# Band attention, SiLU feed-forward and a top-1 mixture of experts in one kernel: the first slots, chunk zero, unit one's transposes and the first expert loads are put in another order

## The chip, the cores and the metric

The kernel runs on one core of a Trainium2 chip. The metric is the device time of one execution in microseconds (us). The kernel before was timed three times: 567.33, 568.43 and 568.99 us, median 568.43 us.

## The reference, cut to what matters

Three stages follow each other on B = 2 sequences of S = 768 tokens, 8 heads of 64 (1536 tokens of 512 values).

```python
# 1 attention: 8 global keys, a local band of 96, a slope per head
scores = q @ k.T / 8 + (-slope[h] * dist)
scores = where(is_global | is_local, scores, -1e9)
a = exp(scores - max); a /= a.sum() + 1e-9
x = (a @ v)                       # 1536 x 512
# 2 feed-forward, 512 -> 2048 -> 512
h = x @ w_in
x = (h * sigmoid(h)) @ w_out
# 3 top-1 mixture of 8 experts, 512 -> 1024 -> 512
e_idx = argmax(x @ w_gate)
y = relu(x[mask] @ w1[e]) @ w2[e]
out[mask] = softmax_weight * sigmoid(x @ w_output_gate)[e] * y
```

## The kernel before

The 1536 tokens are 12 tiles of 128 (n = 0 to 11) and six units of two tiles. Attention is cut into **slots**: slot s = 4n + hp does the two heads 2hp and 2hp+1 of tile n. Slots 0 to 23 (`slot_b`) run ahead of the feed-forward, with fp32 matrix products: the scores (`emit_qk`, L173), scores plus the bias table with their maximum on VectorE (`emit_tb`, L183), the exponential on ScalarE (`emit_exp`, L194), three slots later the transposes (`emit_tr`, L213) and their copies out of PSUM (`emit_cp`, L219 on VectorE, L220 on ScalarE), and one slot after that the product with the values (`emit_px`, L230). At a tile's end the row sums are inverted (`emit_rs`), spread over 512 columns by GpSimd (L1014, `rx`), transposed (`emit_rb`, L237), copied by ScalarE (L239, `xn`) and multiplied into the result (`emit_xx`); GpSimd writes the feed-forward's input from it (`put_xt`, L277 and L279). Slots 24 to 47 (`slot`) run inside the feed-forward, with fp16 pairs (`emit_h` L198, `emit_l` L201 and L204, a DMA transpose on SyncE's queue, `emit_pv` L254, `emit_fin` L264, `emit_xt` L271, then L278 and L279).

The bias tables are built at the very start. `params` asks for the two band sizes, `spread` converts them (L89) and copies them to all partitions with a small matmul (`pfb`, L91) and L92; `table_floats` converts index grids (L116 on VectorE, L117 on ScalarE); `table` makes three VectorE steps (L123 to L125), once for the 128-wide slice of a sequence's first tile and once for the other three slices (384 wide); `tab_heads` scales a table for a head, even heads on ScalarE (L129) and odd ones on VectorE (L128). TensorE is kept at work meanwhile by `warm` (L83), matmuls of a matrix of ones whose result nothing reads.

The feed-forward runs in five chunks of 16 steps: chunk 0 has units 0 and 1, chunks 1 to 4 one unit each. Step g does the first product (`s1_mm`, L355, 12 matmuls a unit), tanh and product (L359, L360), the split into two parts (`s1_sp`, L363 on ScalarE, L364 on VectorE), and two steps later the second product (`s2_mm`, L375 to L377, with `wolr` tiles that `load_wol`, L344, fetches). Everything else is put between these by the step loop (L1093 to L1145), an order written out by hand: slots put their parts in a list that `run_ev` empties, gating functions sit in a list that `run_gates` empties one a step. `slot_b` of drain slots 24 to 27 (the last slots' tails) falls in the first steps of chunk 0; `gate_consts` (L387 to L405, constants on GpSimd and the load of `wgs`) stands ahead of chunk 0. A unit of chunks 1 to 3 is turned for gating by `turn`, which sets two DMA transposes (L439, L440) on SyncE's queue per tile; `gate3` ranks tokens by small matmuls (L477 to L479) and `gate4` scatters rows into expert order (L500).

In chunk 4 `moe2_pre` asks step by step for the first 16 tiles of expert weights (`load_u`, L563, 256 KB each) and splits them (`split_u`: L568 on ScalarE, L569 on VectorE); `early_load` (L577, L579) fetches the first expert's rows after the scatter. All these loads and the `wolr` ones are issued by SyncE, in order. Then `moe2` runs the experts.

Of the kernel before, what the change touches and what calls it, by code (L numbers as in the profile page):

```python
# [17 lines left out]
ALU = mybir.AluOpType  # L18
# [5 lines left out]
def kernel(ctx, tc, qk, v, n_global, n_local, w_in, w_out, wg, w1, w2, out):  # L24
# [33 lines left out]
    tabs=attn.tile([P,4,H,P],BF16,name="tabs")  # L58
# [54 lines left out]
    def table_floats(k,e):  # L113
        w,ii,jj=tabm['w']
        for o,i in ((w[:,0,k],ii[:,k]),(w[:,1,k],jj[:,k])):
            if e is V: V.tensor_copy(o,i)  # L116
            else: A.activation(out=o,in_=i,func=AF.Copy)  # L117
    def table(k):

        w=tabm['w'][0]  # L120
        rel,col,loc,a=(w[:,i,k] for i in range(4))
        ng=pf[:,0:1]; nl=pf[:,2:3]
        V.tensor_scalar(out=loc,in0=rel,scalar1=nl,scalar2=BIG,op0=ALU.is_ge,op1=ALU.mult)  # L123
        V.scalar_tensor_tensor(out=loc,in0=col,scalar=ng,in1=loc,op0=ALU.is_ge,op1=ALU.mult)
        V.scalar_tensor_tensor(out=a,in0=rel,scalar=nl,in1=loc,op0=ALU.min,op1=ALU.add)  # L125
    def tab_heads(dst,src,hs):
        for h in hs:
            if h%2 if dst.start<3 else h<2: V.tensor_scalar(out=tabs[:,dst,h,:],in0=tabm['w'][0][:,3,src],scalar1=-8.0*2.0**-(h+1),scalar2=None,op0=ALU.mult)  # L128
            else: A.activation(out=tabs[:,dst,h,:],in_=tabm['w'][0][:,3,src],func=AF.Copy,scale=-8.0*2.0**-(h+1))  # L129

    atags=[['a','s20','s21','s22','s23']]; acnt=[0]; ded=[False]
# [4 lines left out]
    raw={}; vraw={}; kb={}; qs={}; vp={}; tt={}; hl={}; pT={}; pvt={}; mx={}; ss={}; xT={}  # L136
    def load(s):
        n,hp=divmod(s,4); b,i=divmod(n,NT); r=ring[hp//2]; z=ksl(n)
        if n==0: A.dma_start(r[:,hp%2,z],qk[b,i,hp//2,:,hp%2])
        elif hp%2==0: S.dma_start(r[:,:,z],qk[b,i,hp//2])  # L140
    def load_v(n):
            b,i=divmod(n,NT)
# [73 lines left out]
    def emit_cp(y,m,e):  # L216
        for r in range(2):
            o=y[:,:,:,r*D:(r+1)*D]
            if e is V: V.tensor_copy(o,m[r])  # L219
            else: A.activation(out=o,in_=m[r],func=AF.Copy)  # L220
# [535 lines left out]
    def moe2_pre(k):  # L756

        q=[(q,i) for q in (0,2,1,3) for i in range(KC)]
        w=(0,0,2,2,2,3,3,1,1,2)
        if 6<=k<16:  # L760
            for _ in range(w[k-6]): split_u(*q[nq[1]],pool=False); nq[1]+=1
            while nq[0]<min(16,nq[1]+4*(k-5),nq[1]+NQR): load_u(*q[nq[0]]); nq[0]+=1
        if k==6: early_iota()
        if k==7: early_load()
        if k==8: early_rows()
        if k==13: early_prep()
# [216 lines left out]
    def own(n): return 4*(n+2)>=SB  # L983
    def slot_b(s):
# [19 lines left out]
        def a2():  # L1004
            if cur: emit_tb(n,hp,1)
            if o3: emit_cp(*cp[0],A if DQ<=s<23 else V)
            if o3 and h3==3 and own(n3): emit_rb(n3)
            if o4: emit_px(n4,h4)
            if o4 and h4==3 and not own(n4): emit_rb(n4)
            if o5 and h5==3 and not own(n5): emit_xx(n5)  # L1010
            if o2 and h2==3:
                for k in range(2): emit_rs(n2,k)
                r=attn.tile([P,512],F32,tag="t",name="rx",bufs=3)
                G.tensor_copy(r.rearrange("p (h d) -> p h d",h=H),rs[n2].to_broadcast([P,H,D])); rs[n2]=r  # L1014
        ev.append(a2)
        def b_():
            if cur: glob_k(n,hp)
            if h4==3 and o4 and own(n4): emit_xx(n4)
            if s==0: table(slice(0,3))
            for d,h in TB.get(s,()): tab_heads(slice(0,2) if d==0 else slice(2,3),slice(0,2) if d==0 else slice(2,3),(h,))  # L1020
            if hp==3 and 4*(n+1)<SB and cur: load_v(n+1)
        ev.append(b_)
# [43 lines left out]
    with tc.manual_schedule():  # L1066
        params()
        want(7); load_v(0)
        table_ints()
        warm(6)  # L1070
        spread()
        warm(2)
        table_floats(slice(3,4),V)
        table(slice(3,4))
        table_floats(slice(0,3),A)
        tab_heads(slice(3,4),slice(3,4),range(H))
        rows_init()
        s=0
        while s<SB:
# [4 lines left out]
            s+=1  # L1084
            for x in WP.get(s,()): w_to(*x)
        atags[0]=['s20','s21','s22','s23']
        gate_consts()

        steps=[(c,f) for c in range(len(CH)) for f in range(FB)]
        pend=[]  # L1090
        gq=[]
# [4 lines left out]
        for g in range(len(steps)+LAG):  # L1096
            live=g<len(steps)
            if live:
# [4 lines left out]
                for u in CH[c]: s1_mm(u,f)  # L1103
                for u in CH[c]: s1_ev(u,f)
                if c==0:
                    for _ in range(2):
                        if s<SB+4: pend+=slot_b(s); s+=1
                    if g==3: atags[0]=['a']
                    if f==FB-1: s=SB
                elif c<4 and s<NS+4 and (f>1 and f!=8 if c==1 else f%2==0):  # L1110
                    pend+=slot(s); s+=1
                run_ev(2 if c<2 else 1)
                for u in CH[c]: s1_sp(u,f)
# [6 lines left out]
            if g>=LAG:  # L1120
# [3 lines left out]
                if f2==FB-1:  # L1124
# [3 lines left out]
                    at=len(gq)  # L1128
                    for u in CH[c2]:
                        seq=[lambda n=n,fn=turn if u in PU else gate1: fn(n) for n in (2*u,2*u+1)]  # L1130
                        if u==1: seq=[lambda n=n,h=h: turn(n,(h,)) for n in (2,3) for h in (0,1)]
                        if u in PU: seq=[lambda u=u,fn=fn: fn(u) for fn in (piece1,piece2,piece3,piece4)]+seq+[lambda: None]*2
                        seq+=[lambda u=u,fn=fn: fn(u) for fn in (gate2,gate3,lambda u: gate4(u,1))]
                        for i,fn in enumerate(seq):
                            if at+i<len(gq): gq[at+i]=lambda fs=(gq[at+i],fn): [f() for f in fs]
                            else: gq.append(fn)
                        at=len(gq)-(4 if u in PU else 0)
# [76 lines left out]
```

## Time and profile before

| what | value |
|---|---|
| median of three runs | 568.43 us |
| the profiled execution | 571.45 us, span of its instructions 569.7 us |
| TensorE matmul busy (PE) | 552.6 us, 97% of the span |
| weight load (PEld) | 469.5 us |
| VectorE (DVE) | 391.0 us |
| ScalarE (ACT) | 302.7 us |
| GpSimd (POOL) | 142.2 us |
| attention ahead of the feed-forward | 0 to about 43 us |
| chunk 0, chunks 1 to 3, chunk 4 | to about 136, 313, 366 us |
| experts | from there to the end |

An engine's busy time is the sum of its instructions' durations. In a row of a timeline the first number is the start, the second the time taken by the group, and the bracket tells how long the engine stood idle before it and what released it. PEld is TensorE's weight load, which runs beside its matmuls. SPq, ACTq and POOLq are the sequencers that issue DMAs.

### The profile page before, as it was taken

The page shows a single profiled execution, that of the slowest core. Times are in us where ns is not written, and L with a number is a line of the kernel's source. Part 1 is how long each engine was busy: PE and PEld are TensorE (multiplying, and loading weights), DVE is VectorE, ACT ScalarE, POOL GpSimd, SP SyncE. Part 2 cuts the span into 40 slices and gives each one's busy share as a digit, 9 for nine tenths or more (in the row PEclk, how much of TensorE's full clock was granted, in tenths as well). Part 3 has the DMA queues.
Part 4 walks back from the last instruction along what each step waited for, and adds up shares of the span by engine and source line. Part 5 has one row for each costly group of instructions (what it writes and reads, how often), then busy time and mean ns, then how long its engine had stood idle before and what let it go on. Part 6 is the DMA issues. An engine that isn't in the chain of part 4 may idle for free.

```text
span 569.7 us, 12001 instructions
## 1 busy us (share of the span) xinstructions
PE 552.6 (97%) x4027; PEld 469.5 (82%) x4027; DVE 391.0 (69%) x1143; ACT 302.7 (53%) x819; POOL 142.2 (25%) x193
## 2 busy tenths in 40 slices
PE   9999999999999999999999999999999999999992
PEld 4667998888888888888998988788887888888871
DVE  6995899996478757574735256647674966977940
ACT  6994444443545454434522325727655776877740
POOL 2686434444133313123201010210011010010011
PEclk9999999999999999999999999999999999999997
DMA  6776477796657986664394349319674867867500
GB/s 221 263 238 198 168 216 231 232 310 217 196 154 172 185 206 154 170 160 146 102 184 129 79 144 337 111 56 339 223 216 143 275 199 238 262 221 260 156 20 23
DMA packets 90731, 107.55 MB, mean 189 GB/s; under 512 B 39180, under 2 KB 53516, under 8 KB 90660
## 3 DMA queue, kind: packets, MB, share of 16 engines
q1 hardware_dynamic: 87892, 99.77, 59.4%
q0 software_dynamic: 2192, 6.39, 3.0%
q8 instruction: 34, 0.56, 0.4%
q10 hardware_dynamic: 576, 0.52, 0.3%
q14 instruction: 37, 0.30, 0.2%
HBM read 87.14 MB, written 17.66 MB: 184 GB/s over the span
## 4 chain that ended last, share of the span: by engine, by line
PE 79%; DMA 5%; DVE 5%; issue 4%; ACT 4%; POOL 1%; SPq 1%; POOLq 0%; DVEq 0%; ACTq 0%
PE s L355 21%; PE s L375 7%; PE s L376 7%; PE s L377 7%; PE h L698 5%; PE xy L173 4%; PE y L731 3%; PE y L732 3%; PE y L733 3%; PE h L699 3%; PE pv L254 2%; PE h L704 2%; PE px L230 1%; PE xy L213 1%; DMA out_dram<-y,ixt 1%
## 5 line engine op out<-in xcount | busy, mean ns | idle before, releaser
L355 PEld LDWEIGHTS s<-xT,wi 128*128 128x128 f32 x1152 | 146.7, 190 | 8.4 <-DVE g L364 3.8
L355 PE MATMUL s<-xT,wi 128*128 128x256 f32 x1152 | 152.9, 284 | 0.5 <-DVE g L364 0.5
L359 ACT ACTIVATE u<-s 128x256 f32<-128x256 f32 x96 | 35.4, 381 | 98.7 <-PE s L355 98.5
L360 DVE SCALAR_TENSOR_TENSOR s<-u,s 128x256 f32<-128x256 f32 x96 | 39.7, 426 | 66.3 <-ACT u L359 66.0
L375 PE MATMUL s<-woh,g 128*128 128x512 f32 x192 | 78.4, 408 | 0.4 <-ACT g L363 0.4
L569 DVE TENSOR_TENSOR uq<-qr,uq 128x512 fp32r<-128x512 f32 x112 | 74.4, 689 | 4.8 <-ACT uq L568 2.8
L376 PE MATMUL s<-woh,g 128*128 128x512 f32 x192 | 75.8, 395 | 0.0
L568 ACT ACTIVATE uq<-qr 128x512 fp32r<-128x512 f32 x112 | 66.6, 625 | 2.7 <-DMA qr<-in_w_dram 2.7
L655 POOL DMA_INDIRECT out_dram<-y,ixt x17 | 18.9, 1114 | 156.8 <-ACT y L744 117.2
L364 DVE TENSOR_TENSOR g<-s,g 128x256 fp32r<-128x256 f32 x96 | 39.1, 421 | 22.0 <-ACT g L363 17.9
L363 ACT ACTIVATE g<-s 128x256 fp32r<-128x256 f32 x96 | 35.6, 381 | 30.2 <-DVE s L360 30.2
L194 ACT ACTIVATE t<-t,mx 128x256 f32<-128x256 f32 (+1 forms) x96 | 46.1, 487 | 0.6 <-DVE mx L183 0.5
L375 PEld LDWEIGHTS s<-woh,g 128*128 128x128 f32 x192 | 36.3, 189 | 7.4 <-issue 1.7
L376 PEld LDWEIGHTS s<-woh,g 128*128 128x128 f32 x192 | 36.3, 189 | 5.5 <-DVE g L364 0.5
L377 PE MATMUL s<-wolr,g 128*128 128x512 f32 x128 | 39.8, 392 | 0.2 <-DMA wolr<-wlo_d 0.2
L711 DVE TENSOR_TENSOR h<-h,hs 128x192 f32<-128x192 f32 (+5 forms) x56 | 20.8, 372 | 25.3 <-ACT hs L710 25.2
L731 PE MATMUL y<-uq,hh 128*128 128x512 f32 (+1 forms) x88 | 36.7, 417 | 0.0
L732 PE MATMUL y<-uq,hh 128*128 128x512 f32 (+1 forms) x88 | 34.6, 393 | 0.0
L733 PE MATMUL y<-uq,hh 128*128 128x512 f32 (+1 forms) x88 | 34.6, 393 | 0.0
L713 ACT ACTIVATE hh<-h 128x192 fp32r<-128x192 f32 (+5 forms) x56 | 19.8, 353 | 26.5 <-DVE h L711 15.9
L698 PE MATMUL h<-xwT,uq 128*128 128x448 f32 (+5 forms) x144 | 32.5, 347 | 0.0
L716 DVE SCALAR_TENSOR_TENSOR hh<-h,hh 128x128 fp32r<-128x128 f32 (+4 forms) x88 | 23.2, 293 | 13.2 <-ACT hh L713 13.2
(271 smaller groups left out, 1041.1 us busy)
## 6 DMA issues: line engine op xcount, KB each, us to landing
qr<-in_w_dram SPq DMA_DIRECT2D x128, 256.0 KB, 4.1
wolr<-wlo_d SPq DMA_DIRECT2D x64, 256.0 KB, 3.3
wiraw<-in_w_in_dram SPq DMA_DIRECT2D x16, 512.0 KB, 5.0
wraw<-in_w_out_dram SPq DMA_DIRECT2D x13, 512.0 KB, 4.0
ring<-in_qk_dram SPq DMA_DIRECT2D x22, 256.0 KB, 3.9
xe<-xe SPq DMA_DIRECT2D x7, 792.0 KB, 6.2
wlo_d<-wol SPq DMA_DIRECT2D x16, 256.0 KB, 2.7
xw<-xe SPq DMA_DIRECT2D x15, 264.0 KB, 4.7
```

Of the source, the lines that this page charges most:

```text
L194: A.activation(out=t[:,j,:ce],in_=t[:,j,:ce],func=AF.Exp,scale=-1.0 if 4*n<SB else 0.125,bias=mx[n][:,h:h+1],accum_out=ss[n][:,h,0:1])
L355: T.matmul(t,w[:,ww,kc,:],x[:,xx,kc,:],start=(k==0),stop=(k==11)); k+=1
L360: V.scalar_tensor_tensor(out=t,in0=u,scalar=1.0,in1=t,op0=ALU.add,op1=ALU.mult)
L375: T.matmul(o,g[u][:,0,sl],wh,start=(f==0),stop=False)
L376: T.matmul(o,g[u][:,1,sl],wh,start=False,stop=False)
L377: else: T.matmul(o,g[u][:,0,sl],wl,start=False,stop=(f==FB-1))
L568: A.activation(out=t[:,0],in_=r,func=AF.Copy)
L569: (G if (i%2 if pool is None else pool) else V).tensor_tensor(out=t[:,1],in0=r,in1=t[:,0],op=ALU.subtract)
L698: for kc in range(KC): T.matmul(t[:,:2*W],uq[4*p+2*(f//4),kc][:,0,s],xwT[p,kc][:,:,:W],start=(kc==0),stop=False)
L731: T.matmul(o,hi,w[:,0],start=(f==0),stop=False)
L732: T.matmul(o,g[:,z:z+n],w[:,0],start=False,stop=False)
L733: T.matmul(o,hi,w[:,1],start=False,stop=(f==7))
```

## The change

The edits fall in five places.

1. **Start.** Four warm matmuls instead of six stand ahead of `spread` and four instead of two behind it; VectorE's conversions L116 go ahead of `spread`. The three steps of the 384-wide table, which stood together in slot 0, go one ahead of slot 0, one into slot 0, one into slot 1. The eight odd-head scalings of these slices move from VectorE to GpSimd. Two of the four first loads of `ring` move from ScalarE's queue to SyncE's.
2. **Slots.** For tiles 4 and 5 `emit_px` is issued ahead of `emit_rb`.
3. **Chunk 0.** The four drain slots come one, two and one to a step instead of two and two, and `gate_consts` is called in step 3.
4. **Chunk 1.** Steps 12 and 15 take no slot (before, step 8), so from there on every slot comes one place later; unit 1's four transposes are issued two at step 12 and two at step 15, instead of one at each of four steps.
5. **Chunk 4.** The limit on the expert tiles asked for is 2(k-4) at step k, where it was 4(k-5) more than the number split.

```diff
-    def table(k):
+    def table(k,steps=(0,1,2)):
...
-        V.tensor_scalar(out=loc,in0=rel,scalar1=nl,scalar2=BIG,op0=ALU.is_ge,op1=ALU.mult)
-        V.scalar_tensor_tensor(out=loc,in0=col,scalar=ng,in1=loc,op0=ALU.is_ge,op1=ALU.mult)
-        V.scalar_tensor_tensor(out=a,in0=rel,scalar=nl,in1=loc,op0=ALU.min,op1=ALU.add)
+        if 0 in steps: V.tensor_scalar(out=loc,in0=rel,scalar1=nl,scalar2=BIG,op0=ALU.is_ge,op1=ALU.mult)
+        if 1 in steps: V.scalar_tensor_tensor(out=loc,in0=col,scalar=ng,in1=loc,op0=ALU.is_ge,op1=ALU.mult)
+        if 2 in steps: V.scalar_tensor_tensor(out=a,in0=rel,scalar=nl,in1=loc,op0=ALU.min,op1=ALU.add)
...
-            if h%2 if dst.start<3 else h<2: V.tensor_scalar(out=tabs[:,dst,h,:],in0=tabm['w'][0][:,3,src],scalar1=-8.0*2.0**-(h+1),scalar2=None,op0=ALU.mult)
+            if h%2 if dst.start<3 else h<2: (G if dst.start<3 else V).tensor_scalar(out=tabs[:,dst,h,:],in0=tabm['w'][0][:,3,src],scalar1=-8.0*2.0**-(h+1),scalar2=None,op0=ALU.mult)
...
-        if n==0: A.dma_start(r[:,hp%2,z],qk[b,i,hp//2,:,hp%2])
+        if n==0: (A if hp<2 else S).dma_start(r[:,hp%2,z],qk[b,i,hp//2,:,hp%2])
...
-            while nq[0]<min(16,nq[1]+4*(k-5),nq[1]+NQR): load_u(*q[nq[0]]); nq[0]+=1
+            while nq[0]<min(16,2*(k-4),nq[1]+NQR): load_u(*q[nq[0]]); nq[0]+=1
...
+            if o4: emit_px(n4,h4)
             if o3 and h3==3 and own(n3): emit_rb(n3)
-            if o4: emit_px(n4,h4)
...
-            if s==0: table(slice(0,3))
+            if s==0: table(slice(0,3),(1,))
+            if s==1: table(slice(0,3),(2,))
...
-        warm(6)
+        warm(4)
+        table_floats(slice(3,4),V)
         spread()
-        warm(2)
-        table_floats(slice(3,4),V)
+        warm(4)
         table(slice(3,4))
         table_floats(slice(0,3),A)
         tab_heads(slice(3,4),slice(3,4),range(H))
+        table(slice(0,3),(0,))
...
-        gate_consts()
-
...
-                    for _ in range(2):
+                    for _ in range(2 if g==1 else 1):
                         if s<SB+4: pend+=slot_b(s); s+=1
-                    if g==3: atags[0]=['a']
+                    if g==3: atags[0]=['a']; gate_consts()
...
-                elif c<4 and s<NS+4 and (f>1 and f!=8 if c==1 else f%2==0):
+                elif c<4 and s<NS+4 and (f>1 and f not in (12,15) if c==1 else f%2==0):
...
-                        if u==1: seq=[lambda n=n,h=h: turn(n,(h,)) for n in (2,3) for h in (0,1)]
-                        if u in PU: seq=[lambda u=u,fn=fn: fn(u) for fn in (piece1,piece2,piece3,piece4)]+seq+[lambda: None]*2
+                        if u==1: seq=[lambda: None,seq[0],lambda: None,lambda: None,seq[1]]
+                        if u in PU: seq=[lambda u=u,fn=fn: fn(u) for fn in (piece1,piece2,piece3,piece4)]+seq+[lambda: None]*(1 if u==1 else 2)
```

On TensorE, at the start, where `pfb` is the matmul that spreads the band sizes, `wm` the warm ones and `xy` the first scores, the order before was:

```order
8 L83 MATMUL wm<-ones 128x512
9 L83 LDWEIGHTS ones
10 L83 MATMUL wm<-ones 128x512
11 L83 LDWEIGHTS ones
12 L83 MATMUL wm<-ones 128x512
13 L91 MATMUL pfb<-pf_136,onef 128x4
14 L83 LDWEIGHTS ones
15 L83 MATMUL wm<-ones 128x512
16 L83 LDWEIGHTS ones
17 L83 MATMUL wm<-ones 128x512
18 L173 MATMUL xy<-ring_76 128x128 x4
```

and with the change it is:

```order
8 L83 MATMUL wm<-ones 128x512
9 L91 MATMUL pfb<-pf_136,onef 128x4
10 L83 LDWEIGHTS ones
11 L83 MATMUL wm<-ones 128x512
12 L83 LDWEIGHTS ones
13 L83 MATMUL wm<-ones 128x512
14 L83 LDWEIGHTS ones
15 L83 MATMUL wm<-ones 128x512
16 L83 LDWEIGHTS ones
17 L83 MATMUL wm<-ones 128x512
18 L173 MATMUL xy<-ring_76 128x128 x4
```

Eight warm matmuls stand ahead of the first scores in both; `pfb` has moved up past two of them.

On TensorE, around the first steps of chunk 0 (`px` is the product with the values, `rb` the transposed row sums, L355 the feed-forward's first product, two rows a step), the order before was:

```order
95 L237 MATMUL rb<-ident,rx 128x128 x4
96 L230 MATMUL px<-pT_796,vpr 64x128 x4
97 L213 MATMUL xy<-ident,t 128x64 x8
98 L230 MATMUL px<-pT_831,vpr 64x128 x4
99 L355 MATMUL s_914<-xT,wi 128x256 x12
100 L355 MATMUL s_927<-xT,wi 128x256 x12
101 L213 MATMUL xy<-ident,t 128x64 x8
102 L230 MATMUL px<-pT_864,vpr 64x128 x4
103 L213 MATMUL xy<-ident,t 128x64 x8
104 L230 MATMUL px<-pT_956,vpr 64x128 x4
105 L355 MATMUL s_994<-xT,wi 128x256 x12
106 L355 MATMUL s_1007<-xT,wi 128x256 x12
```

and with the change:

```order
95 L230 MATMUL px<-pT_796,vpr 64x128 x4
96 L237 MATMUL rb<-ident,rx 128x128 x4
97 L213 MATMUL xy<-ident,t 128x64 x8
98 L230 MATMUL px<-pT_831,vpr 64x128 x4
99 L355 MATMUL s_883<-xT,wi 128x256 x12
100 L355 MATMUL s_896<-xT,wi 128x256 x12
101 L213 MATMUL xy<-ident,t 128x64 x8
102 L230 MATMUL px<-pT_864,vpr 64x128 x4
103 L355 MATMUL s_941<-xT,wi 128x256 x12
104 L355 MATMUL s_954<-xT,wi 128x256 x12
105 L213 MATMUL xy<-ident,t 128x64 x8
106 L230 MATMUL px<-pT_925,vpr 64x128 x4
```

`px` has moved ahead of `rb`, and one pair of transposes and product has moved from ahead of step 1's L355 rows to behind them.

On SyncE's queue in chunk 4 (`qr` is a tile of expert weights, `ex` and `exg` the scattered rows, an ISA row the register work ahead of an address), the order before was:

```order
173 L563 ISA
174 L563 DMA qr<-in_w_dram 128x512
175 L563 ISA
176 L563 DMA qr<-in_w_dram 128x512
177 L577 ISA
178 L577 DMA ex<-xe 128x528
179 L579 ISA
180 L579 DMA exg<-xe 128x2x528
181 L344 DMA wolr<-wlo_d 128x512
182 L563 ISA
183 L563 DMA qr<-in_w_dram 128x512
```

and with the change, where the rows shown begin at the earlier `wolr`:

```order
172 L344 DMA wolr<-wlo_d 128x512
173 L563 ISA
174 L563 DMA qr<-in_w_dram 128x512
175 L563 ISA
176 L563 DMA qr<-in_w_dram 128x512
177 L577 ISA
178 L577 DMA ex<-xe 128x528
179 L579 ISA
180 L579 DMA exg<-xe 128x2x528
181 L344 DMA wolr<-wlo_d 128x512
182 L563 ISA
183 L563 DMA qr<-in_w_dram 128x512
```

Ahead of `ex` there were eight `qr` requests and there are now six; the seventh and eighth have moved behind `exg` and a `wolr`.

## Rows read from the trace of the kernel before

**Rows 1.** The page, part 1: busy time, share of the span, instructions.
```profile
PE 552.6 (97%) x4027; PEld 469.5 (82%) x4027; DVE 391.0 (69%) x1143; ACT 302.7 (53%) x819; POOL 142.2 (25%) x193
```

**Rows 2.** Timeline of TensorE, start: start, time taken, engine, line, operation, count.
```profile
3.81 0.58 PE L91 MATMUL pfb<-pf,onef 1*128 1x4 f32 x2
...
5.29 1.23 PE L173 MATMUL xy<-ring 64*128 64x128 f32 x8
...
9.85 0.84 PE L83 MATMUL wm<-ones 128*128 128x512 bf16 x2
...
10.80 0.65 PE L173 MATMUL xy<-ring 64*128 64x256 f32 x4
```

**Rows 3.** Timeline of TensorE, 40 to 356 us: groups with idle time ahead.
```profile
42.00 0.66 PE L237 MATMUL rb<-ident,rx 128*128 128x128 f32 x4 [0.78 <-POOL rx L1014]
...
48.89 0.66 PE L230 MATMUL px<-pT,vpr 128*64 128x128 f32 x8 [0.22 <-DVE pT L219]
...
53.65 0.66 PE L237 MATMUL rb<-ident,rx 128*128 128x128 f32 x4 [0.65 <-POOL rx L1014]
...
55.79 3.13 PE L355 MATMUL s<-xT,wi 128*128 128x256 f32 x24 [0.46 <-DVE g L364]
...
195.43 0.36 PE L254 MATMUL pv<-vpr,pT 128*128 128x64 bf16 x7 [1.16 <-DVE xa L264]
...
253.59 0.17 PE L477 MATMUL gr<-geb,upper 128*128 128x8 bf16 x1 [0.43 <-DVE xT L279]
...
353.22 0.73 PE L377 MATMUL s<-wolr,g 128*128 128x512 f32 x2 [0.17 <-DMA wolr<-wlo_d]
```

**Rows 4.** Timeline of VectorE, start.
```profile
3.05 0.16 DVE L89 CAST pf<-pi 1x4 f32<-1x4 int32 x1 [1.82 <-DMA pi<-in_n_local_dram]
...
11.48 0.49 DVE L219 COPY pT<-xy 128x128 f32<-128x128 f32 x2 [0.92 <-PE xy L213]
```

**Rows 5.** Line L128 by source: count, duration ns min/median/max, first and last start.
```profile
L128 DVE TENSOR_SCALAR tabs<-wk x10: 175/223/292, 5.9 to 17.6; 128x128 bf16<-128x128 f32 x6, 128x256 bf16<-128x256 f32 x4
```

**Rows 6.** Timeline of ScalarE, 12 to 18 us.
```profile
17.35 0.60 ACT L239 ACTIVATE xn<-rb 128x512 f32<-128x512 f32 x1 [0.85 <-PE rb L237]
```

**Rows 7.** Timeline of GpSimd, 41 to 57 us.
```profile
48.93 0.21 POOL L388 MEMSET upper<- 128x128 bf16 x1
...
51.73 0.24 POOL L402 CAST wgb<-wgs 128x64 bf16<-128x64 f32 x1 [0.79 <-DMA wgs<-in_wg_dram]
...
52.99 0.61 POOL L1014 COPY rx<-rs 128x512 f32<-128x512 f32 x1
```

**Rows 8.** Windows, chunk 0 after 62 us: busy us by engine, granted clock, DMA share, GB/s.
```profile
62.00:136.00 74.00, 74.00 (x466) 65.35 (x465) 68.52 (x126) 31.94 (x76) 31.15 (x24) 1.00 0.71 225
```

**Rows 9.** Timeline of all engines, 250.5 to 254 us.
```profile
251.14 0.64 PE L271 MATMUL ms<-ident,xa 128*128 128x128 f32 x4
...
252.86 0.68 DVE L279 TENSOR_TENSOR xT<-ms,xT 128x512 fp32r<-128x512 f32 x1
...
253.74 0.48 PE L355 MATMUL s<-xT,wi 128*128 128x256 f32 x2
253.84 1.26 SPq L204 DMA_TRANSPOSE pT<-hl  x1
```

**Rows 10.** Timeline of SyncE's queue, 337.5 to 349.5 us: start, time to issue.
```profile
340.75 2.54 SPq L563 DMA_DIRECT2D qr<-in_w_dram  x4
346.06 0.33 SPq L577 DMA_DIRECT2D ex<-xe  x1
```

**Rows 11.** Windows, in chunk 4; columns as above.
```profile
344.00:350.00 6.00, 6.00 (x39) 5.45 (x38) 4.87 (x13) 3.77 (x9) 0.00 (x0) 1.00 1.05 362
```

**Rows 12.** Timeline of ScalarE, 349 to 356 us.
```profile
353.85 0.63 ACT L568 ACTIVATE uq<-qr 128x512 fp32r<-128x512 f32 x1 [2.15 <-DMA qr<-in_w_dram]
```

**Rows 13.** Lines L183 and L198 of VectorE by source: count, duration ns min/median/max.
```profile
L183 DVE CUSTOM_DVE_ANT_1 t<-xy,tabs x40: 370/416/432, 12.1 to 42.8; 128x256 f32<-128x256 f32 x40
...
L198 DVE CAST hl<-t x24: 284/422/1418, 151.8 to 287.3; 128x512 f16<-128x512 f32 x20, 128x256 f16<-128x256 f32 x4
```

## The prediction

> **What bounds the kernel now.** Read the page's busy times first. TensorE's matmuls take 552.6 of the span's 569.7 us [rows 1]; so the time moves only by the 17.1 us in which TensorE does nothing, or by stretches in which its work runs slowly. The change adds and removes no matmul (eight warm ones precede the first scores before and after). So I went through TensorE's timeline and listed, at the places that the change touches, its waits and who ends them. One slow stretch exists: at the start eight score matmuls of 128 columns take 1.23 us, and from 10.80 four of 256 columns, as many columns, take 0.65 [rows 2]. That is TensorE's lower clock level, 1.2 GHz, then the upper, 2.4 GHz. The waits later on are few and short: 0.78, 0.22, 0.65 and 0.46 us around chunk 0's first steps, 1.16 and 0.43 us in chunks 1 and 2, 0.17 us in chunk 4 [rows 3]. Their sum, 3.87 us, is about the most that the moved slots and loads can win; the start has its own account.
>
> A difference under 0.3%, 1.7 us, could hardly be told from none in a measurement of this kernel.
>
> **Start.** `pfb` stood behind six warm matmuls at 3.81 us; its input was ready at 3.21 (a cast at 3.05, 0.16 long) [rows 2, 4]. Behind four it starts at about 3.3. From `pfb` to the first scores were 5.29 - 3.81 = 1.48 us, with two warm matmuls between; two more, 0.42 each (two take 0.84), make 2.32 [rows 2]. The first scores come at 3.3 + 2.32 = 5.62 or a little after, 0.35 to 0.45 later. From there until after 10 us TensorE runs in order without a gap at the lower level, so the delay would be kept, except that the clock rose there and work pushed past that point takes half its time: about 0.2 is left at the first transposes. Behind them VectorE stood idle 0.92 us before the copies at 11.48 [rows 4], which now start near 11.7.
>
> Against it stands the relief of VectorE: the eight odd-head scalings go to GpSimd. Ten of them have a median of 0.223 us [rows 5]; eight make 1.8, of which by their starts some 1.3 fell after 11.48, where VectorE runs without a gap. But the gain ends where ScalarE takes over: its first row-sum copy, at 17.35, had stood 0.85 us idle for TensorE [rows 6], and from there ScalarE itself has no gap until the attention ends, so that VectorE's relief is worth nothing more. By then about two scalings lay on VectorE's path, 0.5. A delay of 0.2 and a relief of 0.5 give **-0.3**. GpSimd takes 0.61 us for a copy of 512 columns [rows 7], so a scaling of 256 takes no more; it has nothing urgent there, and eight, at most 4.9 us over seven slots, are covered. Were one in the way, the row-sum copy would be late by 0.6. The three steps of the table, moved apart, end before GpSimd is asked; the two `ring` loads change queues well ahead of their use: both nothing. Ends: -1.4 (all 0.85 us goes, and a score group of 1.23 runs at the upper level, 0.6 less) and +0.5 (the delay stays whole).
>
> **Chunk 0.** `px` ahead of `rb` fills the first gap with 0.66 us of work that was ready. The wait of 0.78 is gone but for 0.1, and step 0 comes 0.7 earlier. What is late next: step 1's product needs a PSUM bank that the split L364 of the step before frees, the releaser of the 0.46 [rows 3]. One slot less now stands ahead of step 1, its product of 0.66, some 0.3 of transposes and the 0.22 of waiting; TensorE gets there about 1.2 us before that release, and waits for it. Behind step 1 stands one slot more, which covers the later `rx` copy. That copy came at 52.99 because GpSimd was in `gate_consts` from 48.93 on, 0.79 us of it a wait for `wgs` [rows 7]. Moved to step 3, these 4.1 us do not stand ahead of `rx`; I leave 0.4 of the 0.65, since exponentials, sums and copy still follow each other, and 0.4 for the copies ahead of a `px`. The constants are then behind GpSimd's weight splits, which keep it busy 31.15 of 74 us [rows 8]: hidden. Without `wgs`'s wait they are 3.3 us; if a step's weights waited for them, up to 3.3 would show. Sum: 0.78 + 0.22 + 0.65 + 0.46 = 2.1 go, 1.2 + 0.4 + 0.4 come back: **-0.1**. Ends: -1.5 (only 0.6 comes back) and +0.5 (the bank also holds up step 2).
>
> **Chunks 1 to 3.** Slots move one place; their matmuls are the same. The wait of 0.43 [rows 3] came from a ranking matmul in a PSUM bank that the input split L279 still read; with slots one place later the two are in different steps: -0.43. The wait of 1.16 was for a tile's result; its two slots stay neighbours, so it stays. New is that a tile's transposes L271 fall in the last step of chunks 2 and 3. From their end, 251.14 + 0.64, to the end of L279, 252.86 + 0.68, are 1.76 us [rows 9], which the next chunk's first product needs in part. Between stand a second product of some 1.4 us and the first four matmuls (two take 0.48 with their tails). Wait 0 to 0.15, twice: +0.1. Unit 1's transposes in pairs hold SyncE's queue 2.5 instead of 1.26 us [rows 9], in steps that take no slot: nothing. Together **-0.4**, ends -1.0 (part of the 1.16 too) and +0.3.
>
> **Chunk 4.** Here I see a cost. SyncE issues in order. Eight requests stood ahead of `ex`, which waits for the scatter until 346.06 [rows 10]; now the seventh and eighth stand behind `ex`, `exg` and a `wolr`. From 344 to 350 the DMA engines are full, 362 GB/s [rows 11], so 256 KB take 262144 B / 362 GB/s = 0.72 us. The `wolr` that TensorE awaited 0.17 us [rows 3] comes two tiles, 1.4 us, sooner: -0.2, or -0.4 with what the wait cost the step behind it. The ninth tile, for which ScalarE stood idle 2.15 us until 353.85 [rows 12], has one `wolr` more ahead of it: +0.7. ScalarE works in order and the next tanh stands behind that split, so the tanh, the PSUM bank that it frees and the matmuls behind come 0.7 later, and the two tiles that moved may add 0.2: +0.9 - 0.3 = **+0.6**. Ends: -0.3 (TensorE has slack for all of it) and +2.3 (the DMA engines run dry before 346.06, and the three late tiles, 3 x 0.72, all show).
>
> **Sum.** -0.3 - 0.1 - 0.4 + 0.6 = -0.2. The profiled execution of 571.45 us becomes 571.25. It lies 3.02 above the median of the runs, 568.43, so the forecast is **568.2**. The experts keep their order on every engine.
>
> **A rule against it.** The scalings go to GpSimd while VectorE has no gap. VectorE's fp16 conversion has a median of 0.42 us and took 1.42 once, with GpSimd's line L153 beside it; its score step stayed within 0.37 to 0.43 in all forty cases, GpSimd at work or not [rows 13]. The Trainium skill (GPSIMD Engine Reference, 8. Key points) says that GpSimd shares its SBUF interfaces with VectorE, and that VectorE's two-port modes and its instructions with two SBUF inputs contend for them. The trace agrees for the conversion; the score step, with one input in PSUM, doesn't show it. By that rule the sum would be higher by each two-input step that a scaling meets; C prices it.
>
> **Rivals.**
>
> *A, faster.* The start wins its whole idle time and chunk 0's waits really go. Start -1.4, chunk 0 -1.5, chunks 1 to 3 -0.4, chunk 4 +0.6 make -2.7: 565.7. For it: ScalarE's 0.85 and three of chunk 0's four waits are attacked by name. Against it: each has another waiter close behind. 0.28.
>
> *B, slower.* The ninth expert tile at ScalarE; it decides once its split ends later than 353.85 + 0.63 + 0.7 = 355.2, because then the PSUM banks of the next steps are held too. Chunk 4 +2.3 in place of +0.6, start +0.2 in place of -0.3: 568.2 + 1.7 + 0.5 = 570.4. For it: 2.15 us of waiting show that ScalarE has no tile in store. Against it: with full DMA engines only the order changes. 0.13.
>
> *C, GpSimd and VectorE hold each other up.* If each of eight scalings stops VectorE for up to 0.6, and a third of that lies on the path, +1.6: 569.8. Forty equal score steps speak against it. 0.05.
>
> *D, the move of the slots only moves waits.* The 0.43 goes, but the two chunk ends wait 0.4 each: +0.7 on the sum, 568.9. The tight 1.76 us speak for it. 0.06.
>
> **How the numbers follow.** The forecast has the remaining 0.48. A lies below 566.7, and the forecast's own spread adds a little: faster 0.30. B and some of C lie above 570.1: 0.15. The rest, 0.55, is within 0.3%. The range goes from A's 565.7, rounded to 565.8, to 570.0, short of B; about 0.18 is outside.
>
> **What would show it.** Right: first scores near 5.7 us and ScalarE's row-sum copy near 17.0; almost no wait at the first `rb` but one of about 1 us at step 1's first product; nothing at the ranking matmul; ScalarE waiting for more than one expert tile in chunk 4, with a longer step behind. Wrong: a score group ahead of 10 us at the upper clock level, waits of TensorE around chunk 0 that sum to under 1 us, a chunk 4 that ends earlier, or a chunk end where L355 waits over 0.4.

## The result, and the profile after

The kernel is slower. Seven runs of the changed kernel have a median of 571.23 us beside 568.23 us for the kernel before: ratio 1.0062, 95% interval 1.0045 to 1.0079 (the two medians alone would give 1.0053). Run again later it gave 570.87 us and 1.0056 (1.0041 to 1.0071). The forecast was 568.2, range 565.8 to 570.0.

The two profiles put side by side hide this, and the reason is the first lesson. The profiled execution of the kernel before took 571.45 us, above all of its 29 runs that were made beside e1 to e4 (566.98 to 570.16); that of the changed kernel took 570.90, within its own runs. So I had the kernel before profiled once more (e1 below, 567.86 us), and read the change against both. The table has the starts of the same instruction, from the timelines of ScalarE; step 4, 8 and 12 are the first tanh (L359) of these steps.

| start, us | before | before, again | changed | e5, only twos | e2, without twos | e15 |
|---|---|---|---|---|---|---|
| first row-sum copy L239 | 17.35 | 16.43 | 15.77 | 16.42 | 15.04 | 14.72 |
| chunk 0, step 4 | 69.92 | 68.79 | 67.99 | 68.91 | 67.32 | 67.01 |
| chunk 4, step 0 | 315.35 | 314.72 | 314.34 | 314.54 | 313.33 | 312.49 |
| chunk 4, step 8 | 340.94 | 340.31 | 339.94 | 340.13 | 338.92 | 338.08 |
| chunk 4, step 12 | 354.39 | 352.38 | 355.61 | 354.80 | 352.23 | 349.37 |
| last scaling L744 | 559.34 | 557.22 | 560.17 | 559.60 | 556.71 | 554.42 |
| span | 569.7 | 566.2 | 569.2 | 568.5 | 565.6 | 563.3 |

Against the second profile the changed kernel leads by 0.66 us at the row-sum copy and by 0.80 in chunk 0, has 0.38 left at chunk 4's step 0, and is 3.23 us behind at its step 12. From step 8 to step 12 it needs 15.67 us; the kernel before needed 13.45 and 12.07. There the time goes, though not all of the difference belongs to the change. The issue of `ex`, which waits for the scatter, moves from run to run: it comes 5.39 us after step 8's tanh in the changed kernel, 5.12 in the first profile of the kernel before and 3.80 in the second. The second one had an early scatter; against the first, the stretch is 2.2 us longer.

The page's part 1 for the changed kernel: TensorE is as busy as before [rows 1]; GpSimd has the eight scalings more.

```profile
PE 552.4 (97%) x4027; PEld 468.7 (82%) x4027; DVE 390.0 (69%) x1135; ACT 302.9 (53%) x819; POOL 147.6 (26%) x201
```

The timeline of TensorE in the changed kernel, the groups that answer to [rows 2] and [rows 3]; the bracket is idle time and what ended it.

```profile
3.25 0.58 PE L91 MATMUL pfb<-pf,onef 1*128 1x4 f32 x2 [0.22 <-DVE pf L89]
...
5.58 1.23 PE L173 MATMUL xy<-ring 64*128 64x128 f32 x8
...
47.05 3.14 PE L355 MATMUL s<-xT,wi 128*128 128x256 f32 x24 [1.20 <-DVE g L364]
...
51.84 0.66 PE L230 MATMUL px<-pT,vpr 128*64 128x128 f32 x8 [0.28 <-DVE pT L219]
52.83 0.66 PE L237 MATMUL rb<-ident,rx 128*128 128x128 f32 x4 [0.33 <-POOL rx L1014]
...
257.69 1.80 PE L355 MATMUL s<-xT,wi 128*128 128x256 f32 x12
...
312.31 1.94 PE L355 MATMUL s<-xT,wi 128*128 128x256 f32 x12
...
352.38 0.73 PE L377 MATMUL s<-wolr,g 128*128 128x512 f32 x2 [0.33 <-DMA wolr<-wlo_d]
...
357.70 0.51 PE L355 MATMUL s<-xT,wi 128*128 128x256 f32 x2 [1.32 <-DVE g L364]
```

The first scores came at 5.58 us (forecast 5.62), the first `rb` no longer waits, step 1's product waits 1.20 us for the bank (forecast 1.2), and the wait at the ranking matmul is gone. New is the last row: a first product in chunk 4 waits 1.32 us. In all, TensorE's waits in chunk 4 sum to 2.0 us in the changed kernel; in the first profile of the kernel before they sum to 0.6, and in the second there are none. What is behind them stands in the timelines of ScalarE and of SyncE's queue in the changed kernel, and in windows of it (columns as in [rows 8]).

```profile
339.94 0.39 ACT L359 ACTIVATE u<-s 128x256 f32<-128x256 f32 x1 [1.56 <-issue]
...
353.04 1.27 ACT L568 ACTIVATE uq<-qr 128x512 fp32r<-128x512 f32 x2 [3.38 <-DMA qr<-in_w_dram]
355.07 0.64 ACT L568 ACTIVATE uq<-qr 128x512 fp32r<-128x512 f32 x1 [0.76 <-DMA qr<-in_w_dram]
355.61 0.36 ACT L359 ACTIVATE u<-s 128x256 f32<-128x256 f32 x1
```

```profile
337.09 1.96 SPq L563 DMA_DIRECT2D qr<-in_w_dram  x4
339.15 0.37 SPq L344 DMA_DIRECT2D wolr<-wlo_d  x1
339.72 0.90 SPq L563 DMA_DIRECT2D qr<-in_w_dram  x2
345.32 0.34 SPq L577 DMA_DIRECT2D ex<-xe  x1
345.90 0.39 SPq L579 DMA_DIRECT2D exg<-xe  x1
346.39 0.41 SPq L344 DMA_DIRECT2D wolr<-wlo_d  x1
347.00 0.86 SPq L563 DMA_DIRECT2D qr<-in_w_dram  x2
```

```profile
344.00:346.00 2.00, 2.00 (x16) 1.89 (x15) 1.46 (x3) 1.81 (x4) 0.00 (x0) 1.00 0.79 301
346.00:348.00 2.00, 2.00 (x15) 1.86 (x14) 1.46 (x4) 1.37 (x3) 0.00 (x0) 1.00 0.79 246
```

SyncE issues nothing from 340.62 to 345.32, while `ex` waits for the scatter. The seventh and eighth tile are asked for at 347.00 and land so late that ScalarE stands idle 3.38 us; the ninth costs another 0.76. The next tanh stands behind them. In the meantime the DMA engines are 79% busy and move 246 to 301 GB/s. In the first profile of the kernel before, where `ex` was still waiting (until 346.06) but eight tiles had been asked for, the first of these windows reads:

```profile
344.00:346.00 2.00, 2.00 (x15) 1.83 (x14) 1.42 (x7) 1.14 (x4) 0.00 (x0) 1.00 1.01 368
```

The same two windows of the kernel before, second profile, with the row of SyncE's queue for its earlier `ex`:

```profile
344.11 0.34 SPq L577 DMA_DIRECT2D ex<-xe  x1
...
344.00:346.00 2.00, 2.00 (x16) 1.89 (x15) 1.45 (x5) 1.47 (x4) 0.00 (x0) 1.00 0.98 351
346.00:348.00 2.00, 2.00 (x14) 1.78 (x13) 1.45 (x5) 1.35 (x4) 0.00 (x0) 1.00 1.04 382
```

and its timeline of ScalarE, where only the ninth tile is waited for, by 0.77 us (2.15 in the first profile, [rows 12]):

```profile
349.93 1.14 ACT L568 ACTIVATE uq<-qr 128x512 fp32r<-128x512 f32 x2
351.85 0.63 ACT L568 ACTIVATE uq<-qr 128x512 fp32r<-128x512 f32 x1 [0.77 <-DMA qr<-in_w_dram]
352.38 0.37 ACT L359 ACTIVATE u<-s 128x256 f32<-128x256 f32 x1
```

### The profile page after: what moved, and what is told of

It reads as the page before. It is cut to its first block, busy times and chain, and to the rows that moved or that the text cites. A ratio compares the mean times of both kernels' runs of the same rounds, so it can differ in the third digit from the quotient of the medians.

```text
span 569.2 us, 12002 instructions
## 1 busy us (share of the span) xinstructions
PE 552.4 (97%) x4027; PEld 468.7 (82%) x4027; DVE 390.0 (69%) x1135; ACT 302.9 (53%) x819; POOL 147.6 (26%) x201
## 4 chain that ended last, share of the span: by engine, by line
PE 72%; DVE 9%; issue 5%; ACT 4%; DMA 4%; POOL 3%; SPq 1%; POOLq 0%; DVEq 0%; ACTq 0%
PE s L355 17%; PE h L698 7%; PE s L375 5%; PE s L376 5%; PE s L377 5%; PE y L731 4%; PE h L699 4%; PE y L732 4%; PE y L733 4%; PE xy L173 3%; PE pv L254 2%; PE h L704 2%; DMA qr<-in_w_dram 2%; PE y L727 2%; PE y L726 1%
## 5 line engine op out<-in xcount | busy, mean ns | idle before, releaser
L355 PEld LDWEIGHTS s<-xT,wi 128*128 128x128 f32 x1152 | 146.7, 190 | 11.6 <-DVE g L364 6.2
L355 PE MATMUL s<-xT,wi 128*128 128x256 f32 x1152 | 153.5, 285 | 2.8 <-DVE g L364 2.5
L359 ACT ACTIVATE u<-s 128x256 f32<-128x256 f32 x96 | 35.4, 380 | 96.3 <-PE s L355 94.4
L201 POOL TENSOR_TENSOR hl<-t,hl 128x512 f16<-128x512 f32 (+1 forms) x18 | 19.5, 1086 | 56.4 <-DVE hl L198 16.2
```

The costliest lines, as they stand in the source:

```text
L355: T.matmul(t,w[:,ww,kc,:],x[:,xx,kc,:],start=(k==0),stop=(k==11)); k+=1
```

## The experiments

Each ratio is to the kernel before, timed beside it. The parts are the five edits of the change; a part undone or alone has that part's lines of the diff.

**The kernel before once more, e1.** No edit.

> This is the kernel before, unchanged. The profiled execution of before took 571.45 us against a median of 568.23 in seven runs; beside the changed kernel's trace its attention ends 1.8 us later and its last output lands 1.4 us later. Theory 1 (that execution was an unlucky one at its two ends, and the kernel before usually starts as the changed one did): ratio 1.000 within 0.2%, and in the new profile the first upper-clock score group lies near 7.6 us instead of 10.8, ScalarE's first row-sum copy before 16.5 instead of 17.35. Rival (the changed start is what won 1.8 us): the new profile again has the upper clock after 10 us and the copy at 17.35.

Measured: 568.38 us, ratio 1.0003 (0.9987 to 1.0018); profiled execution 567.86. Theory 1 held. TensorE's first eight score matmuls took 0.71 us, in the first profile 1.23 [rows 2]: the upper clock level came before them here. The row-sum copy came 0.92 us earlier with it. Timelines of TensorE and of ScalarE in e1:

```profile
5.22 0.71 PE L173 MATMUL xy<-ring 64*128 64x128 f32 x8
```

```profile
16.43 0.60 ACT L239 ACTIVATE xn<-rb 128x512 f32<-128x512 f32 x1 [0.73 <-PE rb L237]
```

The end of the first profile was long too. Its last output was issued 2.64 us after the last scaling, behind a wait for an earlier output; here it took 1.26 us. Timelines of GpSimd, the first profile and the second:

```profile
561.98 0.94 POOL L655 DMA_INDIRECT out_dram<-y,ixt  x1 [4.31 <-DMA out_dram<-y,ixt]
```

```profile
558.48 0.94 POOL L655 DMA_INDIRECT out_dram<-y,ixt  x1 [2.94 <-DVE y L745]
```

**One part undone, e2 to e4.** In the changed kernel, e2 puts back the limit of the loads, e3 chunk 1, e4 the start.

```diff
-            while nq[0]<min(16,2*(k-4),nq[1]+NQR): load_u(*q[nq[0]]); nq[0]+=1
+            while nq[0]<min(16,nq[1]+4*(k-5),nq[1]+NQR): load_u(*q[nq[0]]); nq[0]+=1
```

> The changed kernel with only the limit on the expert tiles asked for put back to 4(k-5) more than those split. Theory 1 (the loads in twos cost what chunk 4 of the two traces shows, 2.2 us, because ScalarE waits 3.38 + 0.76 us for tiles behind the scatter): 2.2 us less than the changed kernel's 571.2, about 569.0, ratio 1.0015; ScalarE again waits about 2.1 us for one tile only. Rival (the loss is in the start): still 571, ratio 1.005.

Measured: 568.31 us, ratio 0.9994 (0.9980 to 1.0007). With this one line undone nothing of the loss is left; chunk 4 from step 8 to 12 takes 13.31 us. That is more than theory 1 said, whose 1.0015 lies outside the interval, and more than the line costs alone (e5).

```diff
-                elif c<4 and s<NS+4 and (f>1 and f not in (12,15) if c==1 else f%2==0):
+                elif c<4 and s<NS+4 and (f>1 and f!=8 if c==1 else f%2==0):
...
-                        if u==1: seq=[lambda: None,seq[0],lambda: None,lambda: None,seq[1]]
+                        if u==1: seq=[lambda n=n,h=h: turn(n,(h,)) for n in (2,3) for h in (0,1)]
```

> The changed kernel with only chunk 1 put back: step 8 skipped instead of 12 and 15, unit 1's transposes one by one. Theory 1 (the slots' move costs 0.8 us: 0.35 and 0.24 at the end of chunk 3, 0.22 at the end of chunk 2, a wolr wait of 0.34 in chunk 1, less 0.6 at the ranking matmul): 0.8 us less, about 570.4, ratio 1.004. Rival (the move of the slots gains the 0.4 us that was forecast): 571.6, ratio 1.006.

Measured: 570.17 us, ratio 1.0029 (1.0015 to 1.0042): the median gained is more than the traces' 0.8 us, but the interval holds theory 1's 1.004. The rival's 1.006 lies outside it.

```diff
-        warm(4)
-        table_floats(slice(3,4),V)
+        warm(6)
         spread()
-        warm(4)
+        warm(2)
+        table_floats(slice(3,4),V)
...
-        table(slice(0,3),(0,))
```

(with the scalings, the table's steps and the `ring` loads where they were.)

> The changed kernel with only the start put back: six and two warm matmuls, the table in one piece, all odd-head scalings on VectorE, four ring loads on ScalarE's queue. Theory 1 (the start moves the time by less than 0.5 us either way): 570.7 to 571.7, ratio 1.0045 to 1.006. Rival (the start is the cost, some 3 us hidden by a lucky execution in the trace): about 568.3, ratio 1.000. Third theory (the start gains the 1.8 us that the two traces differ by): 573, ratio 1.0085.

Measured: 571.56 us, ratio 1.0057 (1.0039 to 1.0074). The start is not the cost.

**Parts alone, e5, e8, e10, e11, e12.** On the kernel before: the twos (e5), chunk 1 (e8), both (e10), the start (e11), chunk 0 (e12). The diff of e5; the others have their part's lines:

```diff
-            while nq[0]<min(16,nq[1]+4*(k-5),nq[1]+NQR): load_u(*q[nq[0]]); nq[0]+=1
+            while nq[0]<min(16,2*(k-4),nq[1]+NQR): load_u(*q[nq[0]]); nq[0]+=1
```

> The kernel before with only the expert tiles asked for in twos. Theory 1 (the seventh and eighth tile stand on SyncE's queue behind ex, which waits for the scatter; this is most of the loss): 2 to 3.5 us slower, ratio 1.0035 to 1.006, and ScalarE idle over 2.5 us for tiles in chunk 4. Rival (the twos cost only together with the other parts, which make chunk 4 start earlier than the scatter allows): less than 1 us, ratio below 1.002.

> The kernel before with only chunk 1's move of the slots and the paired transposes. Theory 1 (the traces' sum of +0.8: waits at the ends of chunks 2 and 3 and for a wolr tile, less the 0.6 at the ranking matmul): 569.2, ratio 1.0014. Rival (it costs 1.9 us, as the changed kernel with this part undone suggests): 570.3, ratio 1.0033. Second rival (-0.4, as forecast): 0.9993.

> The kernel before with the twos and chunk 1's move, nothing else. Theory 1 (they add): 1.8 + 0.6 = 2.4 us, 570.7, ratio 1.0042. Rival (they strengthen each other): 3.5 to 4.5 us, ratio 1.006 to 1.008.

> The kernel before with only the changed start. Theory 1 (tables ready 0.9 us earlier start ScalarE earlier, and VectorE's block of table steps between the first two slots is gone: ScalarE's first row-sum copy 1.4 us earlier, and nothing takes it back): 567.0, ratio 0.9975. Rival (it is taken back before the end): 568.3, ratio 1.000.

> The kernel before with only px ahead of rb, the drain slots one, two, one, and gate_consts in step 3. Theory 1 (the waits move: TensorE waits 1.2 us at step 1 where it waited 2.1 in four places, and the rest comes back): 568.3, ratio within 0.9985 to 1.001. Rival (a gain of 0.7 to 1.5 us): 567.2, ratio 0.998.

| kernel | median us | ratio | 95% interval |
|---|---|---|---|
| e5, twos | 570.00 | 1.0031 | 1.0019 to 1.0043 |
| e8, chunk 1 | 568.67 | 1.0011 | 1.0000 to 1.0022 |
| e10, twos and chunk 1 | 569.92 | 1.0035 | 1.0022 to 1.0049 |
| e11, start | 567.80 | 0.9994 | 0.9982 to 1.0005 |
| e12, chunk 0 | 568.78 | 1.0017 | 1.0006 to 1.0029 |

The four parts sum to 0.0031 + 0.0011 - 0.0006 + 0.0017 = 0.0053, 3.0 us, against 0.0056 to 0.0062 for the whole. For the twos and chunk 1 together e10 shows no extra. That all parts simply add is not shown: e2 holds the start, chunk 0 and chunk 1, which alone sum to +0.0022, and it measured -0.0006. e5's expectation had 2 us as its low end; 1.8 is just under it. ScalarE's wait came as that theory said, 2.42 + 0.72 us in the timeline of e5:

```profile
352.28 1.27 ACT L568 ACTIVATE uq<-qr 128x512 fp32r<-128x512 f32 x2 [2.42 <-DMA qr<-in_w_dram]
354.26 0.63 ACT L568 ACTIVATE uq<-qr 128x512 fp32r<-128x512 f32 x1 [0.72 <-DMA qr<-in_w_dram]
```

Theory 1 held for e8 and e10. For e11 it missed, and the rival, that the start's gain is taken back, lies within the interval. e12 came out slower than both of its theories.

**The changed kernel again, e9.** No edit to the changed kernel.

> The changed kernel, unchanged, beside the parts. Undoing one part of it saved 3.9 us (loads), 1.9 us (chunk 1) and 0.3 us (start), while the loads and chunk 1 alone cost 1.8 and 0.6 us. Theory 1 (the parts add up: start and chunk 0 -0.9, chunk 1 +0.6, loads +1.8 to +2.6): 569.8 to 570.7, ratio 1.0025 to 1.004, and the seven first runs were on the high side. Rival (the parts strengthen each other in chunk 4): 571.3 to 572, ratio 1.005 to 1.0065.

Measured: 570.87 us, ratio 1.0056 (1.0041 to 1.0071), between the two theories in time and within the rival's ratio. The sum of the parts alone, 0.0053, comes close to it without any strengthening; e2, where undoing the twos gave back more than they cost alone, leaves the question open.

**Where the queue's wait stands, e6, e13, e14.** The edit of e6 on the changed kernel and of e14 on the kernel before is the first line; e13 has the twos and the second.

```diff
-        if k==7: early_load()
+        if k==9: early_load()
```

```diff
-        if k==7: early_load()
+        if k==8: early_load()
```

> The changed kernel with early_load (ex, exg) called at step 9 of chunk 4 instead of step 7: the tiles are still asked for in twos, but none of the first ten stands behind the wait for the scatter. Theory 1 (it is the queue's order behind that wait, not the number asked for at once): the loss goes, about 568, ratio 0.997 to 1.000, and ScalarE waits under 1 us for tiles. Rival (two at a time are too few to keep the DMA engines busy, wherever ex stands): still 570 to 571, with ScalarE waiting over 2 us.

Measured: 567.83 us, ratio 0.9989 (0.9978 to 1.0001). With nothing but `ex` moved, all the changed kernel's loss is gone while the tiles are still asked for in twos. ScalarE's timeline of e6, tiles seven to nine in one go with no wait:

```profile
347.93 1.14 ACT L568 ACTIVATE uq<-qr 128x512 fp32r<-128x512 f32 x2
350.54 1.66 ACT L568 ACTIVATE uq<-qr 128x512 fp32r<-128x512 f32 x3
```

> The kernel before with the tiles asked for in twos, and early_load at step 8 instead of 7, so that again eight tiles stand ahead of the wait for the scatter. Theory 1 (the place behind the wait is the cost): no slower than before, ratio 0.997 to 1.0005. Rival (two at a time are too few): 1.002 to 1.003, as with the twos alone.

Measured: 568.80 us, ratio 1.0014 (1.0001 to 1.0028): between the two. ScalarE's wait for the ninth tile is 0.94 us, between the 2.15 and 0.77 of the kernel before, and step 8 to 12 takes 12.24 us. By the ratios about half of the cost goes with the place in the queue, and the interval leaves room for all or little of it; a rest may lie in the number in flight. In e6 the later `ex` also takes away what the kernel before already paid; e7 below, which differs from e6 by chunk 1 and the twos, is faster by 0.0011, which is what chunk 1 costs alone, so with `ex` at step 9 no cost of the twos is left to see.

> The kernel before with only early_load at step 9 instead of 7, so that ten tiles stand ahead of the wait. Theory 1 (the ninth tile's wait, 0.8 to 2.2 us in four traces of kernels that ask as before, goes): 1.0 to 2.0 us faster, ratio 0.9965 to 0.998. Rival (the gain of the kernel without chunk 1's move and the twos came from the start): 0.9995 to 1.0005.

Measured: 567.98 us, ratio 0.9992 (0.9981 to 1.0003). Twelve tiles stood ahead of `ex` here, not the ten expected. The ninth tile's wait is gone from the trace, but the time shows 0.5 us and not 1.0 to 2.0. The forecast had priced ScalarE's wait, and TensorE had slack for part of it: from step 8's tanh to the end of chunk 4's last second product takes 24.18 us in e14, and the same in e8, e12 and e18, which ask as before. The nine profiles that ask as before average 24.96, so by the traces there were 0.8 us to win.

**Combinations, e7 and e15.** e7 is the kernel before with the changed start, chunk 0 and `early_load` at step 9; e15 is the same without chunk 0.

> The kernel before with the changed start and chunk 0, ex and exg asked for at step 9, and neither the twos nor the move of the slots. By the traces so far: start -1.2 (ScalarE's first row-sum copy at 15.04 against 16.43 where the upper clock came equally early), chunk 0 about 0, ScalarE's wait for the ninth tile gone (-0.5 to -1): 566.5, ratio 0.9965. Rival (the start's gain is taken back before the end): 568, ratio 0.999.

> The kernel before with the changed start and early_load at step 9. If the parts add: start -0.3 and early_load -1.0 to -2.0 give 566.0 to 567.0, ratio 0.996 to 0.998. Rival (chunk 0's edits were needed for the gain of 1.25 us): 0.998 to 1.000.

Measured: e7 567.03 us, 0.9978 (0.9967 to 0.9989); e15 566.79 us, 0.9976 (0.9961 to 0.9992). Both are faster than the kernel before and than the changed one; e7 lies between its two theories, e15 within its first. Step 8 to 12 takes 11.45 and 11.29 us.

**Chunk 0 in its edits, e16 to e18.** On the kernel before, `gate_consts` in step 3 alone, the drain slots alone, `px` ahead of `rb` alone.

```diff
-        gate_consts()
...
-                    if g==3: atags[0]=['a']
+                    if g==3: atags[0]=['a']; gate_consts()
```

> The kernel before with gate_consts called in step 3 of chunk 0, the drain slots two and two and rb ahead of px as before. Theory 1 (chunk 0's cost was not its own: traces within 0.1 us): ratio 0.9985 to 1.001. Rival (the constants behind GpSimd's weight splits delay something that the waits don't name): 1.0015 to 1.003.

```diff
-                    for _ in range(2):
+                    for _ in range(2 if g==1 else 1):
```

> The kernel before with only the four drain slots one, two and one to a step. Theory 1 (this edit makes TensorE wait 1.2 us for the PSUM bank at step 1's product and so takes back what the others give): a wait of about 1 us at that product, chunk 0 left 0.3 to 0.7 us later, ratio 1.0005 to 1.0025. Rival (the waits only change places): ratio 0.999 to 1.0005.

```diff
+            if o4: emit_px(n4,h4)
             if o3 and h3==3 and own(n3): emit_rb(n3)
-            if o4: emit_px(n4,h4)
```

> The kernel before with only px ahead of rb. Theory 1 (it fills the first gap and step 0 comes 0.6 us earlier, but TensorE meets a later wait): ratio 0.999 to 1.0005, and of the 0.78 us at the first rb at most 0.2 left in the trace. Rival (it costs, since the row-sum copy then stands later on ScalarE): 1.0005 to 1.002.

Measured: 567.70 us, 0.9990 (0.9978 to 1.0002); 569.71 us, 1.0022 (1.0011 to 1.0032); 568.05 us, 0.9996 (0.9983 to 1.0008). All three lie within the ratios of theory 1, and one edit of the three costs. TensorE's timeline of e17 has the wait that the forecast put at step 1, and a longer one than before at the second `rb`:

```profile
49.41 3.14 PE L355 MATMUL s<-xT,wi 128*128 128x256 f32 x24 [1.20 <-DVE g L364]
...
55.19 0.66 PE L237 MATMUL rb<-ident,rx 128*128 128x128 f32 x4 [1.27 <-POOL rx L1014]
```

The second wait is for `rx`, which in e17 itself waited 1.72 us for VectorE's row sums; in the changed kernel, with `px` first and `gate_consts` moved, TensorE's wait there is 0.33 us. So e17 does not tell what the drain slots cost inside the change. From the first row-sum copy to step 4 of chunk 0, e17 takes 53.81 us, the kernel before 52.36 and 52.57; e16 takes 51.87 and e18 51.83.

## Why the prediction was wrong

**Chunk 4 is the step that failed: +0.6 forecast, +1.8 measured (e5, interval 1.1 to 2.4).** "Against it: with full DMA engines only the order changes" was the argument against rival B, and so the forecast took +0.6 of its +2.3. The engines were full in [rows 11] with eight tiles asked for; with six they were at 79% in the windows that matter (81 and 80% in e5, where only the twos are changed), and the tiles not asked for then came late. I also priced only the ninth tile. The seventh and eighth, now behind the wait, cost 3.38 us of ScalarE's time where they had cost none. The `wolr` that was to come sooner and win 0.3 is waited for 0.33 us, where it had been 0.17. Undone, the twos give back 2.9 us by the medians (e2), 3.5 to 3.9 by the ratios; why this is more than they cost alone stays open.

In the traces, step 8 to 12 takes 13.7 to 15.7 us, mean 14.7, in six profiles with the twos and `ex` at step 7, and 11.3 to 14.3, mean 12.6, in nine that ask as before: 2.1 us. Part of the spread is the scatter's: the later `ex` is issued, the longer the stretch. Among the profiles with `ex` 4.5 to 5.4 us after step 8's tanh, five with the twos take 14.8 us on average and six that ask as before 13.1, still 1.7 us apart.

The mechanism of rival B, in-order SyncE, late tiles, in-order ScalarE, held PSUM bank, is what the rows show; I gave it 0.13. The prediction even had it among its signs, more than one tile waited for and a longer step behind, and its end of +2.3 was near; its centre leaned on a resource being full after the change as it was before. The Trainium skill (DMA: Bandwidth & Descriptors, Anatomy of one DMA — SWDGE (gpsimd) path) says that DMA engines do not wait on semaphores and that the wait happens on the issuing sequencer. The trace agrees: 4.7 us without an issue on SyncE's queue, and e6, which moves only the waiting request, takes the loss away.

Chunk 4's is not the only term that was too low: by the parts alone it was short by 1.2 us, chunks 1 to 3 by 1.0 and chunk 0 by 1.1, the last one in doubt, as told below.

**Chunks 1 to 3: -0.4 forecast, +0.6 measured (e8).** The ranking matmul's wait went, as said. "Wait 0 to 0.15, twice" was too small: the first product of chunk 4 takes 1.94 us in the changed kernel and 1.59 elsewhere, and it starts another 0.24 later behind the product ahead of it; the one of chunk 3 takes 1.80. So 0.59 and 0.21 came where +0.1 stood. The chain from L271 to the end of L279, which I measured as 1.76 us, has VectorE's and ScalarE's own work of the step ahead of it (2.13 us at the end of chunk 3 in the changed kernel), and no slot's work covers it. The wait at `pv` stayed, as forecast. From the last tanh of chunk 0 to the first of chunk 4, seven profiles with the moved slots average 182.2 us, thirteen without 181.8.

**Chunk 0: -0.1 forecast.** The trace follows it wait by wait (1.20, 0.28, 0.33 for 1.2, 0.4, 0.4), and from the first row-sum copy to the last tanh of chunk 0 the kernel before again (e1), e12 and the changed kernel are within 0.15 us of each other. What I did not see is that the -0.1 is a sum of unlike parts: alone, two edits gain 0.2 to 0.6 us each by ratios whose intervals hold 1, and 0.5 to 0.7 by the traces, and the third, the drain slots, costs 1.2 (e17). The timing of the three together (e12, +1.0 us by its ratio) is higher than its trace, and e7 and e15, which differ by these edits, are equal; that stays open.

**Start: -0.3 forecast, -0.3 measured (e11, interval -1.0 to +0.3).** The size agrees, partly by luck; the way to it was wrong. The row-sum copy, forecast 0.35 us earlier, comes at 15.65 us on average in the eight profiles with the changed start and at 16.74 in the twelve without; and e15, which differs from e14 by the start alone, is 0.9 us faster. An earlier `pfb`, and VectorE's conversions ahead of it, make the table ready 0.9 us earlier, and ScalarE, which waits for it in both, begins its scalings at 4.99 instead of 5.87 in two profiles with an early upper clock, e2 and then e1:

```profile
4.99 1.30 ACT L129 ACTIVATE tabs<-wk 128x128 bf16<-128x128 f32 x6 [0.65 <-DVE wk L125]
...
5.87 1.30 ACT L129 ACTIVATE tabs<-wk 128x128 bf16<-128x128 f32 x6 [0.69 <-DVE wk L125]
```

From 7.94 us on ScalarE runs without a gap in e2, past the row-sum copy, so it is the path there. GpSimd's scalings were dearer than my bound of 0.61, and hidden as forecast. Groups of GpSimd in e2, 5 to 18 us (busy us, mean ns):

```profile
L128 POOL TENSOR_SCALAR tabs<-wk 128x256 bf16<-128x256 f32 x4 | 3.4, 849 | 3.8 <-DVE wk L125 3.7
L128 POOL TENSOR_SCALAR tabs<-wk 128x128 bf16<-128x128 f32 x4 | 2.1, 528 | 0.1
```

VectorE's score steps of 256 columns beside them took 0.41 us, as without [rows 13]; rival C did not happen. The fp16 conversion that the prediction took as its example needed 1.42 us twice, not once, both times with L153 on GpSimd.

**The base.** Subtracting 3.02 us for the profiled execution was right as a shift, but it hid where the extra time lay. Against e1 it was 0.9 us at the start, 1.4 at the end, and 1.4 from step 8 to 12 of chunk 4, one of the places compared: the 2.15 us of [rows 12] are 0.77 in e1, where the scatter was done earlier.

## What to carry to other kernels

When a request on an in-order queue waits for something slow, count how many useful requests stand ahead of it: moving two behind it cost 1.8 us here, while the rest of the change won nothing clear of noise (e2), and moving the waiting request two steps later gave the loss back. A resource that is full in the trace of before may be full because of what the change takes away. Test edits of a bundle one by one: here one of three neighbours in chunk 0 cost 1.2 us alone while the other two showed no cost. A kernel with the start, `gate_consts`, `px` first and the later `early_load` was not run.

## What was not expected of the hardware

The time at which TensorE's upper clock level begins differed between executions of one kernel: with the same order of matmuls ahead, the first eight score matmuls took 1.23 us in the first profile of the kernel before and 0.71 in the second, and the row-sum copy moved by 0.9 us. The time from the issue of the last scatter to the issue of `ex`, which waits for it, was 6.49, 5.44 and 6.41 us in the two profiles before and the one after, so that the same requests come early or late for the tiles' due times from run to run.
